# Delta-rule attention and a rational MoE on one core: units of 512 elements become pairs of 1024, in one tile with two buffers

## The chip, the cores and the metric

The kernel runs on one core of a Trainium2 chip. The metric is the device time of one execution in microseconds (us), taken as the median of several executions. A profiled execution gives the trace that is read here. The engines are PE (matrix products), DVE (elementwise work), ACT (elementwise functions), POOL (a second elementwise engine) and SP, which issues most DMA transfers. Each engine works through its own list of instructions in order; an instruction that waits for a semaphore holds everything behind it on its engine.

## The reference

The attention part is a delta rule over 768 steps for 4 batches of 8 heads of 48 dimensions, in float32. Its output, reshaped to 3072 tokens of 384, goes through one layer with a rational function:

```python
for t in range(S):
    kt, vt, bt = (k_n[:, :, t], v[:, :, t], beta[:, :, t, None])
    y[:, :, t] = np.einsum('bhd,bhde->bhe', q[:, :, t], state)
    v_old = np.einsum('bhde,bhd->bhe', state, kt)
    state = state + bt[:, :, :, None] * np.einsum('bhd,bhe->bhde', kt, vt - v_old)
...
h = x @ w_in                       # 384 x 2048
P = a[0] + a[1] * h + a[2] * h2 + a[3] * h3
Q = 1.0 + np.abs(b[0]) * np.abs(h) + np.abs(b[1]) * h2
g = P / (Q + 1e-06)
return (g @ w_out).astype(np.float32)   # 2048 x 384
```

The two weight matrices arrive as 64-bit words.

## The kernel before, in words

**Stages.** Up to about 150 us the kernel loads the weights and computes the first attention chunk. `load_in` and `load_out` call `to_f32` (L305 to L325) for each group of 256 or 192 columns: a DMA into a staging tile that shares buffers with the tiles `mw`, `mu` and `mr`, ACT Abs (L316), POOL min and max (L317), DVE shift and mask (L318) and two DVE merges (L325). After that each weight is split into two float16 parts (`split16`, L226 to L232).

**Units.** The attention runs in 12 chunks of 64 steps. A chunk yields 256 tokens, and its MoE work is cut into 8 units of 256 of the 2048 hidden columns, so that there are 96 units. A unit is a set of tiles of 128 partitions by 512 elements:

- `hidden(n)`: 18 products of 128x256 on PE (L808) into one PSUM bank, tile `ph`; the pool `ps_h` has two such banks.
- `numerator(n)`: ACT Abs into `mr` (L826) and ACT Identity into `mu` (L828), both from `ph`; DVE `mw` from `mr` and `ph` (L830); ACT Abs of `mw` (L831); DVE `mu` times `ph` (L832) and the last step of the polynomial (L833).
- `quotient(n)`: ACT Ln (L841) and Exp (L842) into `mr`, the reciprocal of the denominator; DVE `mg` first part (L844); DVE `mw` times that part, written into the PSUM tile `ph` of the *next* unit (L845); DVE the remainder into `mu` (L846); POOL `mg` second part, the product of `mu` and `mr` (L847).
- `accumulate(n)`: 12 products of 128x384 on PE (L862). After the eighth unit of a chunk the sums are copied out (L876) and sent (L884).

**Order.** In the program the loop of `kernel` issues numerator(n), quotient(n-1), a step of the attention, accumulate(n-2) and hidden(n+1). `in_order` ties the six DVE operations of the units to one another in that order, so DVE's list holds L830, L832, L833 of unit n and then L844, L845, L846 of unit n-1. All else is placed by the framework's planner, which puts attention instructions between them where its own time estimate finds room. The attention of chunk c+1 to c+4 runs beside the units of chunk c; it ends before the units do, and the last units run with nothing beside them.

**Buffers.** `mr`, `mu`, `mw` and `mg` have three buffers each: the tile of unit n is the tile of unit n-3 again. Writing into a buffer waits for the last reader of what was there.

Of the kernel before, what the change touches and what calls it, by code (L numbers as in the profile page):

```python
# [36 lines left out]
def kernel(  # L37
# [271 lines left out]
    def to_f32(t, src, nm, keep=MIN_NORMAL):

        n = t.shape[-1]
        st = staged([P, n, 2], U32, "ws" + nm)
# [4 lines left out]
        nc.gpsimd.tensor_scalar(a, a, 3.0e38, keep, op0=ALU.min, op1=ALU.max)  # L317
        nc.vector.tensor_scalar(  # L318
            t, a.bitcast(U32), 3, KEEP, op0=ALU.logical_shift_left, op1=ALU.bitwise_and
        )  # L320
        for word, scalar, in1, op0, op1 in (
            (wh, 0xC0000000, t, ALU.bitwise_and, ALU.bitwise_or),
            (wl, 29, t, ALU.logical_shift_right, ALU.bitwise_or),
        ):
            nc.vector.scalar_tensor_tensor(out=t, in0=word, scalar=scalar, in1=in1, op0=op0, op1=op1)  # L325
# [714 lines left out]
```

## Time and profile before

| what | value |
|---|---|
| median of 3 runs | 843.07 us (842.95 to 843.18) |
| profiled execution, its own time | 849.25 us |
| its span on the core | 845.5 us |
| granted PE clock, mean | 0.944 |
| DVE, PE, ACT, POOL busy | 88%, 74%, 73%, 40% of the span |
| first numerator (L830 of unit 0) | starts at 150.29 us |
| L830 of unit 72 | starts at 719.16 us |
| last DVE operation of a unit (L846 of unit 95) | starts at 837.33 us, takes 0.75 |

Rows of the trace read as follows: in a group, the line in the source, the engine, the operation, the tiles written and read, the shape, and the count; then the busy time, the mean duration in ns, and the idle time of the engine just before these instructions with what ended it. In a timeline, the start in us, the duration, the engine and the operation, and in brackets the idle time before it. The table of windows gives, for stretches of the span, each engine's busy time with its number of instructions in brackets, PE's granted clock, the share of the DMA engines that was busy and the rate.

### The profile page before, as it was taken

Reading aid. Unit: us, or ns where it says so; the run is one execution under the profiler, and the core shown is the slowest. Engines: PE = TensorE matmul, PEld = TensorE weight load, DVE = VectorE, ACT = ScalarE, POOL = GpSimd, SP = SyncE. Lnnn points to the kernel's source line nnn. Section 1 sums busy time; section 2 is a strip of 40 time slices with the busy share of each in tenths; the row PEclk is TensorE's granted clock in tenths of the full one; section 3 lists DMA queues with packets and bytes.
Section 4 is the critical chain, followed back from the end, with each engine's and each line's share of the span. In section 5 each row is a group of like instructions: output and inputs, shape, how many; then the busy total and the mean of one; then the engine's idle time right before and its main releaser. Section 6 shows DMA issues by size and latency. Waiting matters only on the chain.

```text
span 845.5 us, 23179 instructions
## 1 busy us (share of the span) xinstructions
PE 627.7 (74%) x9264; PEld 493.8 (58%) x9264; DVE 740.2 (88%) x1405; ACT 617.1 (73%) x1278; POOL 338.1 (40%) x322
## 2 busy tenths in 40 slices
PE   0330346778778777866978988789789789999995
PEld 0220344666566666755866866667567667786662
DVE  5999896688879778987998999989988799998996
ACT  4866658768667675866966968768668768788873
POOL 6545754334435333253433433432433332222232
PEclk9999996898989898989999999989899999999999
DMA  8998979769979879999599399696597674300000
GB/s 237 249 212 170 225 155 170 123 140 169 157 130 165 146 120 191 146 140 183 93 145 187 71 176 150 119 193 105 98 167 111 110 103 80 76 2 21 1 19 19
DMA packets 466507, 111.46 MB, mean 132 GB/s; under 512 B 431328, under 2 KB 463072, under 8 KB 466400
## 3 DMA queue, kind: packets, MB, share of 16 engines
q1 hardware_dynamic: 464224, 108.83, 71.3%
q8 instruction: 72, 1.18, 0.6%
q10 hardware_dynamic: 2176, 1.17, 0.5%
q14 instruction: 35, 0.29, 0.1%
HBM read 40.47 MB, written 26.23 MB: 79 GB/s over the span
## 4 chain that ended last, share of the span: by engine, by line
DVE 34%; PE 19%; DMA 17%; SPq 11%; ACT 10%; issue 7%; POOL 1%; ACTq 0%; DVEq 0%; POOLq 0%
PE ph L808 7%; PE po L862 5%; DVE ph L845 4%; DVE w_out L325 4%; DVE mg L844 3%; DVE mw L830 3%; DVE mu L833 3%; DVE mu L832 3%; SPq L119 3%; PE pu L401 2%; DMA tq<-xdq 2%; DMA gd<-g 2%; DMA tk<-xdk 2%; SPq L475 2%; DVE mu L846 2%
## 5 line engine op out<-in xcount | busy, mean ns | idle before, releaser
L862 PE MATMUL po<-w_out,mg 128*128 128x384 f16 x1152 | 226.5, 339 | 33.3 <-DVE mg L844 20.9
L847 POOL TENSOR_TENSOR mg<-mu,mr 128x512 f16<-128x512 f32 x96 | 124.8, 1300 | 258.1 <-DVE mu L846 203.8
L808 PE MATMUL ph<-xT,w_in 128*128 128x256 f16 x1728 | 216.3, 280 | 14.1 <-DVE mu L846 11.2
L808 PEld LDWEIGHTS <-w_in 128*128 128x128 f16 x1728 | 169.8, 101 | 51.1 <-DVE mu L846 14.4
L862 PEld LDWEIGHTS <-mg 128*128 128x128 f16 x1152 | 109.5, 101 | 103.4 <-DVE mg L844 27.7
L401 PEld LDWEIGHTS <-kbd 128*128 128x128 f16 x1680 | 66.7, 109 | 47.8 <-issue 43.3
L830 DVE SCALAR_TENSOR_TENSOR mw<-mr,msc,ph 128x512 f32<-128x512 f32 x96 | 71.1, 741 | 22.1 <-ACT mu L828 21.9
L831 ACT ACTIVATE mw<-mw 128x512 f32<-128x512 f32 x96 | 60.4, 629 | 39.7 <-DVE mw L830 39.2
L845 DVE SCALAR_TENSOR_TENSOR ph<-mw,msc,mg 128x512 f32<-128x512 f32 x96 | 81.4, 848 | 1.0
L844 DVE SCALAR_TENSOR_TENSOR mg<-mu,msc,mr 128x512 f16<-128x512 f32 x96 | 81.1, 844 | 0.0
L826 ACT ACTIVATE mr<-ph,msc 128x512 f32<-128x512 f32 x96 | 65.2, 679 | 18.7 <-PE ph L808 6.9
L828 ACT ACTIVATE mu<-ph,coef,msc 128x512 f32<-128x512 f32 x96 | 74.2, 773 | 0.0
L846 DVE SCALAR_TENSOR_TENSOR mu<-mu,msc,ph 128x512 f32<-128x512 f32 x96 | 71.1, 741 | 1.4
L833 DVE SCALAR_TENSOR_TENSOR mu<-mu,msc,ph 128x512 f32<-128x512 f32 x96 | 70.7, 736 | 1.0
L841 ACT ACTIVATE mr<-mw,msc 128x512 f32<-128x512 f32 x96 | 69.2, 721 | 1.7
L401 PE MATMUL pu<-z,ebd 128*128 128x48 f16 x1728 | 54.9, 185 | 18.1 <-DVE z L232 13.5
L401 PEld LDWEIGHTS <-ebd 128*128 128x128 f16 x1728 | 53.9, 98 | 21.7 <-issue 19.4
L832 DVE TENSOR_TENSOR mu<-ph,mu 128x512 f32<-128x512 f32 x96 | 65.5, 682 | 0.0
L842 ACT ACTIVATE mr<-mr 128x512 f32<-128x512 f32 x96 | 60.3, 628 | 1.3
L401 PEld LDWEIGHTS <-wbd 128*128 128x128 f16 x1152 | 37.7, 99 | 35.9 <-issue 34.8
L230 POOL TENSOR_TENSOR mm<-m,mm 128x1024 f16<-128x1024 f32 x12 | 29.2, 2436 | 73.6 <-ACT mm L226 64.5
L401 PE MATMUL pm<-tq,kbd 128*128 128x64 f16 x576 | 27.0, 220 | 20.1 <-DMA tq<-xdq 18.3
(195 smaller groups left out, 1195.0 us busy)
## 6 DMA issues: line engine op xcount, KB each, us to landing
...
```

The source lines that it names most:

```text
L401: nc.tensor.matmul(dst[p][:, h], head(bd, lp, p * H + h), head(rt, rp, p * H + h), start=start and n == 0 and h == 0, stop=stop and n == l ...
L808: nc.tensor.matmul(ph[:, i], w_in[:, f2, wp, cc, i * P : (i + 1) * P], x[:, xp, cc], start=k == 0, stop=k == 3 * NCC - 1,)
L828: nc.scalar.activation(u, ph, AF.Identity, scale=A3, bias=a2)
L830: in_order(nc.vector.scalar_tensor_tensor(out=w, in0=z, scalar=B0, in1=ph, op0=ALU.add, op1=ALU.mult))
L832: in_order(nc.vector.tensor_mul(u, ph, u))
L833: in_order(nc.vector.scalar_tensor_tensor(out=u, in0=u, scalar=A1, in1=ph, op0=ALU.add, op1=ALU.mult))
L841: nc.scalar.activation(r, w, AF.Ln, bias=Q0)
L844: in_order(nc.vector.scalar_tensor_tensor(out=g[:, 0], in0=u, scalar=A0, in1=r, op0=ALU.add, op1=ALU.mult))
L845: in_order(nc.vector.scalar_tensor_tensor(out=t, in0=w, scalar=Q0, in1=g[:, 0], op0=ALU.add, op1=ALU.mult))
L846: in_order(nc.vector.scalar_tensor_tensor(out=u, in0=u, scalar=A0, in1=t, op0=ALU.add, op1=ALU.subtract))
L847: nc.gpsimd.tensor_mul(g[:, 1], u, r)
L862: nc.tensor.matmul(po[p], g[:, gp, i, p * P : (p + 1) * P], w_out[:, f2, wp, i], start=f2 == lo and i == 0 and k == 0, stop=f2 == hi - 1 a ...
```

## The change

Two units become one pair, from the first product on. There are 48 pairs. `hidden(m)` makes 36 products into one PSUM tile of two banks, and `ps_h` has one such tile instead of two of one bank. The elementwise steps of a pair are 128x1024, so each is one instruction where it was two. `mr`, `mu` and `mw` are parts of one tile `mx` of 3x1024 elements with two buffers (12 KB per partition each), and `mg` has two buffers. `L845`'s product is written into `mw` in SBUF (now L838) instead of the PSUM tile of the next unit. Ln and Exp are issued with the numerator. The products of both units of pair m-1 are issued at the end of step m. The scales of the columns are per pair, so per 512 columns. The weights' words come in groups of 768 columns, are converted in place, and their staging tile is `mx`. The second half of each `w_out` unit is split by ACT and DVE, not by ACT and POOL.

New lines answer to old ones thus: the products of L808 and L862 become L797 and L855; L826, L828, L830, L831, L832, L833 become L819, L820, L821, L822, L823, L824; L841, L842 become L825, L826; L844, L845, L846, L847 become L837, L838, L839, L840. (So L826 is Abs before and Exp after.) Lines of the attention stand 13 lower (L655 is L642, L705 is L692).

```diff
-    MB = 3
+    MB = 2
-    ps_h = ctx.enter_context(tc.tile_pool(name="ps_h", bufs=2, space=PSUM))
+    ps_h = ctx.enter_context(tc.tile_pool(name="ps_h", bufs=1, space=PSUM))
...
+    NS = NU // 2
-    sw = cpool.tile([P, 4, NU], F32, name="sw")
-    tab = cpool.tile([P, 6, NU], F32, name="tab")
+    sw = cpool.tile([P, 4, NS], F32, name="sw")
+    tab = cpool.tile([P, 6, NS], F32, name="tab")
...
-    def to_f32(t, src, nm, keep=MIN_NORMAL):
+    def to_f32(t, srcs, nm, keep=MIN_NORMAL):
-        st = staged([P, n, 2], U32, "ws" + nm)
-        nc.sync.dma_start(out=st.rearrange("p f w -> p (f w)"), in_=src)
-        a = sb.tile([P, n], F32, tag="mg", name="wa" + nm, bufs=MB)
...
+        st = sb.tile([P, len(srcs), n, 2], U32, tag="mx", name="ws" + nm, bufs=MB)
+        for h, src in enumerate(srcs):
+            w, x = st[:, h], t[:, h]
+            nc.sync.dma_start(out=w.rearrange("p (a f) w -> p a (f w)", a=src.shape[1]), in_=src)
+            wl, wh = w[..., 0], w[..., 1]
+            nc.scalar.activation(x.bitcast(F32), wh.bitcast(F32), AF.Abs)
+            nc.gpsimd.tensor_scalar(x.bitcast(F32), x.bitcast(F32), 3.0e38, keep, op0=ALU.min, op1=ALU.max)
+            nc.vector.tensor_scalar(x, x, 3, KEEP, op0=ALU.logical_shift_left, op1=ALU.bitwise_and)
+            for word, scalar, op0 in ((wh, 0xC0000000, ALU.bitwise_and), (wl, 29, ALU.logical_shift_right)):
+                nc.vector.scalar_tensor_tensor(out=x, in0=word, scalar=scalar, in1=x, op0=op0, op1=ALU.bitwise_or)
...
     def load_out(...):
-        for j in range(2):
-            if j == 0:
-                split16((w_out[:, i, 0, j], w_out[:, i, 1, j]), to[j].bitcast(F32), ss[:, 1:2])
-            else:
-                scaled(to[j].bitcast(F32), ss[:, 1:2])
-                split16((w_out[:, i, 0, j], w_out[:, i, 1, j]), to[j].bitcast(F32), eng=nc.gpsimd)
+        for i in us:
+            split16((w_out[:, i, 0], w_out[:, i, 1]), t[:, i % 2], ss[:, 1:2])
...
-    def hidden(n):
-        ph = ps_h.tile([P, 2, TG], F32, tag="h", name=f"ph_{n}")
+    def hidden(m):
+        ph = ps_h.tile([P, 2, 2, TG], F32, tag="h", name=f"ph_{m}")
+        for h in range(2):
+            for i in range(2):
...
     def numerator(...):
-        r = z = sb.tile([P, 2, TG], F32, tag="mr", name=f"mr{n}", bufs=MB)
-        u = sb.tile([P, 2, TG], F32, tag="mu", name=f"mu{n}", bufs=MB)
-        w = sb.tile([P, 2, TG], F32, tag="mw", name=f"mw{n}", bufs=MB)
+        x = d["x"] = sb.tile([P, 3, 4 * TG], F32, tag="mx", name=f"mx{m}", bufs=MB)
+        u, w, r = (x[:, i] for i in range(3))
...
+        nc.scalar.activation(r, w, AF.Ln, bias=Q0)
+        nc.scalar.activation(r, r, AF.Exp, scale=-1.0)

     def quotient(...):
-        t = unit[min(n + 1, NCH * NU - 1)]["ph"]
-        nc.scalar.activation(r, w, AF.Ln, bias=Q0)
-        nc.scalar.activation(r, r, AF.Exp, scale=-1.0)
-        g = sb.tile([P, 2, 2, TG], F16, tag="mg", name=f"mg{n}", bufs=MB)
-        in_order(nc.vector.scalar_tensor_tensor(out=t, in0=w, scalar=Q0, in1=g[:, 0], op0=ALU.add, op1=ALU.mult))
-        in_order(nc.vector.scalar_tensor_tensor(out=u, in0=u, scalar=A0, in1=t, op0=ALU.add, op1=ALU.subtract))
-        nc.gpsimd.tensor_mul(g[:, 1], u, r)
+        g = d["g"] = sb.tile([P, 2, 2, 2, TG], F16, tag="mg", name=f"mg{m}", bufs=2)
+        in_order(nc.vector.scalar_tensor_tensor(out=w, in0=w, scalar=Q0, in1=g0, op0=ALU.add, op1=ALU.mult))
+        in_order(nc.vector.scalar_tensor_tensor(out=u, in0=u, scalar=A0, in1=w, op0=ALU.add, op1=ALU.subtract))
+        nc.gpsimd.tensor_mul(g1, u, r)
...
-    for n in range(N + 2):
-        c, j = divmod(n, NU)
-        if n < N:
-            numerator(n)
-        if 0 <= n - 1 < N:
-            quotient(n - 1)
-        attention(*divmod(n + SHIFT, NU))
-        if 0 <= n - 2 < N:
-            accumulate(n - 2)
-        if n + 1 < N:
-            hidden(n + 1)
+    for m in range(N // 2 + 1):
+        if m < N // 2:
+            numerator(m)
+        if m > 0:
+            quotient(m - 1)
+        attention(*divmod(2 * m + SHIFT, NU))
+        if m + 1 < N // 2:
+            hidden(m + 1)
+        attention(*divmod(2 * m + 1 + SHIFT, NU))
+        if m > 0:
+            accumulate(2 * m - 2)
+            accumulate(2 * m - 1)
...
+    nc = _bacc.Bacc("TRN2", target_bir_lowering=False, num_devices=1, dynamic_dma_scratch_size=2048)
```

The order of instructions moves with it. In the rows below a name is a tile with its number, what stands ahead of `<-` is written, `msc` and `coef` are scales, and the brackets name the engines whose semaphores the instruction waits for.

DVE at the end of the program, where no attention is left. Before:

```order
L830 SCALAR_TENSOR_TENSOR mw90_13819<-mr90_13815,msc_11_13589,ph_90_13796 128x512 [waits PE_49,Activation_49]
L832 TENSOR_TENSOR mu90_13817<-ph_90_13796,mu90_13817 128x512 [waits Pool_49]
L833 SCALAR_TENSOR_TENSOR mu90_13817<-mu90_13817,msc_11_13589,ph_90_13796 128x512 [waits DVE_49]
L844 SCALAR_TENSOR_TENSOR mg89_13826<-mu89_13765,msc_11_13589,mr89_13763 128x512
L845 SCALAR_TENSOR_TENSOR ph_90_13796<-mw89_13767,msc_11_13589,mg89_13826 128x512 [waits DVE_49]
L846 SCALAR_TENSOR_TENSOR mu89_13765<-mu89_13765,msc_11_13589,ph_90_13796 128x512 [waits DVE_49]
L830 SCALAR_TENSOR_TENSOR mw91_13868<-mr91_13864,msc_11_13589,ph_91_13845 128x512 [waits PE_49,Activation_49]
```

and with the change:

```order
L821 SCALAR_TENSOR_TENSOR mx45_12531<-mx45_12531,msc_11_12350,ph_45_12465 128x1024 [waits PE_49,Activation_49,Pool_49]
L823 TENSOR_TENSOR mx45_12531<-ph_45_12465,mx45_12531 128x1024
L824 SCALAR_TENSOR_TENSOR mx45_12531<-mx45_12531,msc_11_12350,ph_45_12465 128x1024 [waits DVE_49]
L837 SCALAR_TENSOR_TENSOR mg44_12540<-mx44_12451,msc_11_12350 128x1024
L838 SCALAR_TENSOR_TENSOR mx44_12451<-mx44_12451,msc_11_12350,mg44_12540 128x1024 [waits DVE_49]
L839 SCALAR_TENSOR_TENSOR mx44_12451<-mx44_12451,msc_11_12350 128x1024 [waits DVE_49]
L821 SCALAR_TENSOR_TENSOR mx46_12608<-mx46_12608,msc_11_12350,ph_46_12545 128x1024 [waits PE_49,Activation_49,Pool_49]
```

The step of three operations for the new tile and three for the tile before stays; L830 waited for PE and ACT, and L821, which opens the step, waits for POOL too.

ACT at the same place. Before, unit 92 and the opening of unit 93:

```order
L826 ACTIVATE mr92_13911<-ph_92_13892,msc_11_13589 128x512 [waits PE_49,Pool_49]
L828 ACTIVATE mu92_13913<-ph_92_13892,coef_99,msc_11_13589 128x512
L831 ACTIVATE mw92_13915<-mw92_13915 128x512 [waits DVE_49]
L841 ACTIVATE mr92_13911<-mw92_13915,msc_11_13589 128x512 [waits Activation_49]
L842 ACTIVATE mr92_13911<-mr92_13911 128x512 [waits Activation_49]
L826 ACTIVATE mr93_13958<-ph_93_13939,msc_11_13589 128x512 [waits PE_49,Pool_49]
L828 ACTIVATE mu93_13960<-ph_93_13939,coef_99,msc_11_13589 128x512
```

and with the change, pair 46 and the opening of pair 47:

```order
L819 ACTIVATE mx46_12608<-ph_46_12545,msc_11_12350 128x1024 [waits PE_49,Pool_49]
L820 ACTIVATE mx46_12608<-ph_46_12545,coef_99,msc_11_12350 128x1024
L822 ACTIVATE mx46_12608<-mx46_12608 128x1024 [waits DVE_49]
L825 ACTIVATE mx46_12608<-mx46_12608,msc_11_12350 128x1024 [waits Activation_49]
L826 ACTIVATE mx46_12608<-mx46_12608 128x1024 [waits Activation_49]
L819 ACTIVATE mx47_12683<-ph_47_12622,msc_11_12350 128x1024 [waits PE_49,Pool_49]
L820 ACTIVATE mx47_12683<-ph_47_12622,coef_99,msc_11_12350 128x1024
```

The order of the five functions is the same. L826 of unit 92 writes the buffer of `mr` that unit 89 used, and the POOL operation that it waits for is L847 of unit 89. L819 of pair 46 writes the buffer of `mx` that pair 44 used, and the POOL operation that it waits for is L840 of pair 44, whose DVE input (L839 of pair 44) stands in DVE's list directly ahead of L821 of pair 46.

DVE in the middle of the program, with attention between (`pr`, `wt0`, `wh`, `S16`, `z`, `sh`, `m32` are its tiles). Before:

```order
L833 SCALAR_TENSOR_TENSOR mu8_3392<-mu8_3392,msc_1_3087,ph_8_3371 128x512 [waits DVE_49]
L844 SCALAR_TENSOR_TENSOR mg7_3401<-mu7_3237,msc_0_1329,mr7_3235 128x512
L571 TENSOR_REDUCE wt0_111<-pr_3_2504 128x2x4x4 [waits DVE_49]
L845 SCALAR_TENSOR_TENSOR ph_8_3371<-mw7_3239,msc_0_1329,mg7_3401 128x512 [waits DVE_49]
L561 TENSOR_TENSOR pr_3_2504<-gb_3_2329,wt0_111 128x512 [waits DVE_49]
L232 SCALAR_TENSOR_TENSOR z_2_1_3406<-pu_2_3144,zmask_85,z_2_1_3406 128x768 [waits Activation_49]
L846 SCALAR_TENSOR_TENSOR mu7_3237<-mu7_3237,msc_0_1329,ph_8_3371 128x512 [waits DVE_49]
L830 SCALAR_TENSOR_TENSOR mw9_3521<-mr9_3517,msc_1_3087,ph_9_3498 128x512
L832 TENSOR_TENSOR mu9_3519<-ph_9_3498,mu9_3519 128x512 [waits Pool_49]
```

and with the change:

```order
L824 SCALAR_TENSOR_TENSOR mx8_3919<-mx8_3919,msc_2_3647,ph_8_3750 128x1024 [waits DVE_49]
L837 SCALAR_TENSOR_TENSOR mg7_3928<-mx7_3678,msc_1_2608 128x1024
L565 SCALAR_TENSOR_TENSOR wh_5_4450<-wt0_111,wh_5_4450 128x256 [waits DVE_49]
L692 SCALAR_TENSOR_TENSOR S16_133<-pd_3_4297,sc_3_1907,S16_133 128x768 [waits PE_49]
L838 SCALAR_TENSOR_TENSOR mx7_3678<-mx7_3678,msc_1_2608,mg7_3928 128x1024 [waits DVE_49]
L232 SCALAR_TENSOR_TENSOR sh_4_4494<-S16_133,sc_4_2959,sh_4_4494 128x768 [waits Activation_49]
L839 SCALAR_TENSOR_TENSOR mx7_3678<-mx7_3678,msc_1_2608 128x1024 [waits DVE_49]
L642 TENSOR_TENSOR m32_5_4226<-pm_5_4177,mask_91 128x1024 [waits DMAHW2_49,DMAHW1_49,PE_49]
L821 SCALAR_TENSOR_TENSOR mx9_4280<-mx9_4280,msc_2_3647,ph_9_4013 128x1024 [waits Activation_49,Pool_49]
L823 TENSOR_TENSOR mx9_4280<-ph_9_4013,mx9_4280 128x1024
```

Attention instructions stand between L821 of a pair and L839 of the pair before as well as between that L839 and the next L821.

More of the change, by code (lines that the diff above doesn't have):

```diff
@@ L785, in scalars @@
         if lo == 0:
-            d["m"] = sb.tile([P, 6, NU], F32, tag="msc", name=f"msc_{c}")
+            d["m"] = sb.tile([P, 6, NS], F32, tag="msc", name=f"msc_{c}")
         nc.vector.tensor_mul(d["m"][:, :, u], tab[:, :, u], sf.unsqueeze(2).broadcast_to([P, 6, hi - lo]))
         d["ikap"][lo] = hi, ikap
-    unit = {}
     acc = {}
@@ L798 @@
     obs = {}
-    def hidden(n):
-        c, f2 = divmod(n, NU)
+    both = {}
+    def hidden(m):
+        c, s2 = divmod(m, NS)
         x = toks[c]["x"]
-        ph = ps_h.tile([P, 2, TG], F32, tag="h", name=f"ph_{n}")
-        for i in range(2):
-            k = 0
-            for cc in range(NCC):
-                for wp, xp in PASSES:
-                    nc.tensor.matmul(
-                        ph[:, i],
-                        w_in[:, f2, wp, cc, i * P : (i + 1) * P],
-                        x[:, xp, cc],
-                        start=k == 0,
-                        stop=k == 3 * NCC - 1,
-                    )
-                    k += 1
-        unit[n] = {"ph": ph}
@@ L818, in numerator @@
-    def numerator(n):
-        c, f2 = divmod(n, NU)
-        d = unit[n]
-        A3, B1, A1, B0, A0, Q0 = (toks[c]["m"][:, i, f2 : f2 + 1] for i in range(6))
-        ph = d["ph"]
-        r = z = sb.tile([P, 2, TG], F32, tag="mr", name=f"mr{n}", bufs=MB)
-        nc.scalar.activation(z, ph, AF.Abs, scale=B1)
-        u = sb.tile([P, 2, TG], F32, tag="mu", name=f"mu{n}", bufs=MB)
+        ph = ps_h.tile([P, 2, 2, TG], F32, tag="h", name=f"ph_{m}")
+        for h in range(2):
+            for i in range(2):
+                k = 0
+                for cc in range(NCC):
+                    for wp, xp in PASSES:
+                        nc.tensor.matmul(
+                            ph[:, h, i],
+                            w_in[:, 2 * s2 + h, wp, cc, i * P : (i + 1) * P],
+                            x[:, xp, cc],
+                            start=k == 0,
+                            stop=k == 3 * NCC - 1,
+                        )
+                        k += 1
@@ L828, in numerator, with flat @@
+        both[m] = {"ph": ph}
+    def flat(t):
+        return t.rearrange("p i a t -> p (i a t)")
+    def numerator(m):
+        c, s2 = divmod(m, NS)
+        d = both[m]
+        A3, B1, A1, B0, A0, Q0 = (toks[c]["m"][:, x, s2 : s2 + 1] for x in range(6))
+        ph = flat(d.pop("ph"))
+        x = d["x"] = sb.tile([P, 3, 4 * TG], F32, tag="mx", name=f"mx{m}", bufs=MB)
+        u, w, r = (x[:, i] for i in range(3))
+        nc.scalar.activation(r, ph, AF.Abs, scale=B1)
         nc.scalar.activation(u, ph, AF.Identity, scale=A3, bias=a2)
-        w = sb.tile([P, 2, TG], F32, tag="mw", name=f"mw{n}", bufs=MB)
@@ L986 @@
                 back(0, j)
-            elif what == "w":
+            elif what == "w" and j < NS:
                 load_in(j)
-            elif what == "o":
+            elif what == "o" and j < NS:
                 weights_out(j)
```

116 lines of the change are left out of this document (52 added, 64 removed).

## The prediction

> **What bounds the kernel now.** I read the page's busy shares, the table of windows by stage, then the timeline of the last stretch, where only units run.
>
> ```profile
> PE 627.7 (74%) x9264; PEld 493.8 (58%) x9264; DVE 740.2 (88%) x1405; ACT 617.1 (73%) x1278; POOL 338.1 (40%) x322
> 0.00:150.00 150.00, 48.64 (x731) 40.73 (x732) 127.52 (x347) 99.52 (x263) 86.31 (x122) 0.95 0.91 201
> 220.00:700.00 480.00, 396.59 (x6229) 314.23 (x6226) 428.12 (x751) 353.10 (x690) 184.62 (x145) 0.94 0.83 140
> 784.90:829.00 44.10, 41.82 (x309) 29.10 (x307) 42.90 (x69) 36.95 (x70) 12.76 (x10) 1.00 0.04 10
> ```
>
> DVE is the fullest engine throughout: 85% of the first 150 us, 89% of the middle, 97% at the end, where POOL is busy for 29%. The rate of units follows from the starts of L826:
>
> ```profile
> 220.00:700.00 480.00, 42.18 (x62) 0.94 0.83 140
> 784.93 0.67 ACT L826 ACTIVATE mr<-ph,msc 128x512 f32<-128x512 f32 x1
> 829.03 0.67 ACT L826 ACTIVATE mr<-ph,msc 128x512 f32<-128x512 f32 x1
> ```
>
> In the middle 62 units take 480 us, 15.5 us for two; at the end ten units lie between these two starts, 8.8 us for two. One round of DVE there:
>
> ```profile
> 790.76 0.75 DVE L846 SCALAR_TENSOR_TENSOR mu<-mu,msc,ph 128x512 f32<-128x512 f32 x1
> 791.42 0.74 DVE L830 SCALAR_TENSOR_TENSOR mw<-mr,msc,ph 128x512 f32<-128x512 f32 x1
> 792.08 0.68 DVE L832 TENSOR_TENSOR mu<-ph,mu 128x512 f32<-128x512 f32 x1
> 792.81 0.74 DVE L833 SCALAR_TENSOR_TENSOR mu<-mu,msc,ph 128x512 f32<-128x512 f32 x1
> 793.47 0.75 DVE L844 SCALAR_TENSOR_TENSOR mg<-mu,msc,mr 128x512 f16<-128x512 f32 x1
> 794.25 0.76 DVE L845 SCALAR_TENSOR_TENSOR ph<-mw,msc,mg 128x512 f32<-128x512 f32 x1
> 795.04 0.75 DVE L846 SCALAR_TENSOR_TENSOR mu<-mu,msc,ph 128x512 f32<-128x512 f32 x1
> ```
>
> L846 to L846 is 4.28 us without a gap: with three buffers POOL and ACT run ahead, and DVE alone sets the pace.
>
> **The change part by part.** *Wider DVE operations.*
>
> ```profile
> L832 DVE TENSOR_TENSOR mu<-ph,mu 128x512 f32<-128x512 f32 x96 | 65.5, 682 | 0.0
> L655 DVE TENSOR_TENSOR m<-pm,mask 128x1024 f32<-128x1024 f32 x12 | 14.6, 1216 | 10.6 <-PE pm L401 10.6
> ```
>
> The second 512 elements cost 1216 - 682 = 0.53 us, the first about 0.71 start to start. Six operations per pair are 4.28 + 6 x 0.53 = 7.48 us instead of 8.56: 1.08 us less per pair, 52 us over 48 pairs, if DVE still set the pace. From the start of the numerator's first to the end of the quotient's last operation it is 3.62 (791.42 to 795.04) + 0.75 + 6 x 0.53 = 7.57 us.
>
> [...]
>
> *Two buffers for a pair.* L819 of pair m+1 writes the `mx` that pair m-1 still holds until POOL's L840 has read it (the rows of pair 46). L840 needs L839 of pair m-1, which stands on DVE behind pair m's numerator. L821 of m+1 then waits for ACT's L819 and L820. So DVE round, POOL and ACT come one after another, where three buffers let them overlap. The prices:
>
> ```profile
> 785.50 0.77 ACT L828 ACTIVATE mu<-ph,coef,msc 128x512 f32<-128x512 f32 x1
> 785.68 0.75 DVE L846 SCALAR_TENSOR_TENSOR mu<-mu,msc,ph 128x512 f32<-128x512 f32 x1
> 786.35 0.74 DVE L830 SCALAR_TENSOR_TENSOR mw<-mr,msc,ph 128x512 f32<-128x512 f32 x1
> 786.60 1.27 POOL L847 TENSOR_TENSOR mg<-mu,mr 128x512 f16<-128x512 f32 x1 [3.69 <-ACT kp L761]
> L230 POOL TENSOR_TENSOR mm<-m,mm 128x1024 f16<-128x1024 f32 x12 | 29.2, 2436 | 73.6 <-ACT mm L226 64.5
> L230 POOL TENSOR_TENSOR kn<-q,kn 128x768 f16<-128x768 f32 x12 | 20.4, 1699 | 9.9 <-ACT kn L226 9.6 <-DMA gb<-gd 0.2
> L516 ACT ACTIVATE g<-pg 128x1024 f32<-128x1024 f32 x12 | 12.3, 1023 | 6.6 <-PE pg L401 5.5 <-POOL nrm L494 1.0
> ```
>
> DVE to POOL is 786.60 - 786.43 = 0.17. L840 at 1024: 2.13 by the line through 1.27 at 512 and 1.70 at 768, 2.54 by doubling; I take 2.34, close to L230's 2436 ns. POOL to ACT as DVE to POOL, 0.17. ACT: L516's 1023 less L826's 0.67 is 0.35 for the second half, so L819 holds ACT for 0.57 + 0.35 = 0.92 (784.93 to 785.50) and L820 takes 0.77 + 0.35 = 1.12; doubled these would be 1.14 and 1.54. ACT to DVE 0.08 (786.27 to 786.35). Loop: 7.57 + 0.17 + 2.34 + 0.17 + 0.92 + 1.12 + 0.08 = **12.4 us** (12.2 to 13.2) against 8.8. DVE would sit idle for 4.8 us of each.
>
> *Behind the waiting L819* stand on ACT the attention's casts and splits (L226, L228) and copies; PE's products for `pu` and DVE's `z` wait for those. L824 is the last reader of the only `ph`, so hidden(m+1) starts there:
>
> ```profile
> 795.94 2.13 PE L808 MATMUL ph<-xT,w_in 128*128 128x256 f16 x18 [0.19 <-DVE kp L780]
> ```
>
> 36 products are 4.27 us, hidden under the quotient, POOL and its latencies (3.9 + 2.7). At the end that holds, so the single PSUM tile and later products cost nothing; uncovered it is a rival. Fewer ACT and POOL instructions save nothing beyond what the loop's prices hold, since both engines wait within it: ACT is at 74%, POOL at 38% in the middle.
>
> *Start (to the first numerator).*
>
> ```profile
> L325 DVE SCALAR_TENSOR_TENSOR w_out<-wso,w_out 128x192 uint32<-128x192 uint32 x56 | 24.3, 449 | 0.4
> L325 DVE SCALAR_TENSOR_TENSOR w_out<-wsi,w_out 128x256 uint32<-128x256 uint32 x48 | 21.8, 469 | 0.3
> L318 DVE TENSOR_SCALAR w_out<-wai 128x256 uint32<-128x256 uint32 x24 | 10.6, 441 | 4.7 <-POOL wai L317 4.7
> L318 DVE TENSOR_SCALAR w_out<-wao 128x192 uint32<-128x192 uint32 x28 | 10.4, 373 | 0.0
> ```
>
> Some 160 instructions (67 us) become 32 of about 0.95 and 16 of 0.56 at 768 elements, 39 us. The 28 us shrink by overlapping ends (L846's 0.75 against 0.66 to the next start: 0.09 x 112 = 10), and the `w_out` split moved from POOL adds 384 elements to each of eight DVE operations, 0.4 x 8 = 3: 15 net, up to 20 if fewer ends overlap. Scales per pair drop some 0.15 us operations, which is within that. But the first numerator also follows a chain through the attention's PE and ACT steps and the gate, in which 22 of the 150 us leave DVE idle already; how much of the saving reaches its end the trace doesn't show, so I take nearer the lower third, -6 (-20 if all counts; +3 if two staging buffers, with transfers of 786 KB instead of 256 and DMA 91% busy, delay loads).
>
> *Pairs 1 to 35.* From L830 of unit 2 to that of unit 72:
>
> ```profile
> 164.60 0.75 DVE L830 SCALAR_TENSOR_TENSOR mw<-mr,msc,ph 128x512 f32<-128x512 f32 x1 [1.52 <-ACT mu L828]
> 719.16 0.75 DVE L830 SCALAR_TENSOR_TENSOR mw<-mr,msc,ph 128x512 f32<-128x512 f32 x1 [1.48 <-ACT mu L828]
> DVE mw L830 <- ACT mu L828: 19.5, 14, 4.2
> DVE m L655 <- PE pm L401: 10.6, 5, 3.7
> DVE ab L545 <- DMA gb<-gd: 7.2, 6, 2.5
> L844 DVE SCALAR_TENSOR_TENSOR mg<-mu,msc,mr 128x512 f16<-128x512 f32 x96 | 81.1, 844 | 0.0
> L845 DVE SCALAR_TENSOR_TENSOR ph<-mw,msc,mg 128x512 f32<-128x512 f32 x96 | 81.4, 848 | 1.0
> L846 DVE SCALAR_TENSOR_TENSOR mu<-mu,msc,ph 128x512 f32<-128x512 f32 x96 | 71.1, 741 | 1.4
> ```
>
> Before: 554.6. After: 35 x 12.4 = 434. The idle 4.8 us can be filled by attention, but 160 of DVE's attention instructions stand within the round (between a pair's L821 and the L839 before it) and lengthen the loop; with their durations (like L655's) they are 74, and where those in the gap exceed it, 8. That gives 516. To it come waits inside the round (in the list of DVE's waits between 160 and 760 us those other than L830's add to some 43 us, L655's and L545's the largest; 43% of the attention's DVE time stands inside the round, so 18; L830's own 19.5 is what the loop now counts), collisions with POOL (L844 and L845, both inputs in SBUF, average 0.1 above L846; three such operations now: 17), and an ACT or POOL late by their own queues (10, an estimate): 561, **+6** (-38 with none of these, +42 with twice as much).
>
> [...]
>
> *Pairs 36 to 47.* Before, 719.16 to 838.08, the last L846's end (next fence): 118.9. After, 11 x 12.4 + the last numerator and quotient 7.6 + a quotient of 3.9 alone + 3 for the last scalars and attention: 151, **+32**.
>
> *The tail.*
>
> ```profile
> 837.33 0.75 DVE L846 SCALAR_TENSOR_TENSOR mu<-mu,msc,ph 128x512 f32<-128x512 f32 x1
> 838.25 1.26 POOL L847 TENSOR_TENSOR mg<-mu,mr 128x512 f16<-128x512 f32 x1 [1.51 <-DVE mu L846]
> 836.80 2.12 PE L862 MATMUL po<-w_out,mg 128*128 128x384 f16 x12 [1.89 <-POOL mg L847]
> ```
>
> POOL is 1.1 longer, and of the last products those that need POOL's part are eight instead of four, 0.18 each: +1 to +3, I take **+3** with the copy behind.
>
> Sum: -6 + 6 + 32 + 3 = **+35**. The profiled execution took 849.25 (span 845.5), 6.2 above the median of 843.07; on the median's scale 843 + 35 = 878.
>
> **The rivals.**
> A, *DVE still sets the pace* (POOL and ACT overlap after all, or the wait on POOL is for an older pair): 52 us saved on units and 6 to 20 at the start, about 780. For it: 97% DVE busy; against: the order of L839, L840, L819, L821, and in the middle DMA, already 83% busy with transfers that don't shrink. Chance 0.06.
> B, *the gap is filled*: attention falls into the idle 4.8 us without lateness (-38), the start keeps its whole -20, the end its +35: about 820 to 838. For it: 428 of 480 us DVE in the middle leaves little idle. Chance 0.11.
> C, *hidden comes late* in PE's queue. PE is busy 396.59 of 480 us, 12.8 per 15.5; 8.5 of that is not hidden. Numerator 3.7 + 4.27 + ACT 2.04 + latencies 0.3 is 10.3, and with three quarters of the others ahead, 6.5, the loop is 16.8: 35 x 16.8 = 588 + 27 for collisions and lateness = 615 against 554.6, +60, about 935. It decides once over 2.1 us of other products stand ahead. Chance 0.10.
> D, the parts cancel, within 0.2%: 0.05.
>
> **How the numbers follow.** The forecast has 0.68, its own range 845 to 912: the bounds leave -14 to +9 around the start's value, -44 to +36 around the middle's, and the loop's -0.2 to +0.8 another -9 to +37 over 46 loops; not all fall together, so I keep some -33 and +34 of them. A, B are faster (0.17), D the same (0.05), forecast and C slower (0.78); 0.2%, 1.7 us, is about what a measurement tells from no change. The range takes in B and the forecast, 830 to 914.
>
> **What would show it.** At the end, L821 starts 12.4 us apart and waits about 4.8 us for ACT, L819 waits for POOL's L840, and DVE's share there falls to about 60%. L840 takes 2.1 to 2.5. L823 takes about 1.2. In the middle two units take 15 to 17 us. If L821 starts 7.5 apart at the end, the loop is wrong; if L819 waits for PE in the middle, C is right; if the first L821 starts before 135 or after 153, the start is.

## The result and the profile after

The changed kernel takes 965.8 us (median of 4 runs, 962.8 to 967.0) against 843.0 us before: 1.146 times, 95% interval 1.142 to 1.149. The direction was forecast; the time lies far above 878 and above the range's 914. The profiled execution has a span of 965.3 us against 845.5, so 119.8 us have to be found.

The page of the kernel after, engines and three groups:

```profile
PE 663.3 (69%) x9264; PEld 518.6 (54%) x9264; DVE 705.9 (73%) x969; ACT 572.1 (59%) x950; POOL 310.8 (32%) x218
L840 POOL TENSOR_TENSOR mg<-mx 128x1024 f16<-128x1024 f32 x48 | 114.2, 2380 | 275.0 <-DVE mx L839 189.3
L821 DVE SCALAR_TENSOR_TENSOR mx<-mx,msc,ph 128x1024 f32<-128x1024 f32 x48 | 61.3, 1278 | 75.3 <-ACT mx L820 65.5
L819 ACT ACTIVATE mx<-ph,msc 128x1024 f32<-128x1024 f32 x48 | 53.3, 1109 | 64.2 <-POOL mg L840 49.3
```

DVE does its work in 436 fewer instructions and 34 us less, and yet its share falls from 88% to 73%: each engine of the loop now waits for another. The table of windows, for the start, pairs 1 to 35 and four pairs of the end:

```profile
0.00:156.00 156.00, 50.45 (x829) 44.12 (x830) 113.81 (x204) 94.51 (x180) 67.60 (x72) 0.93 0.95 201
173.50:800.00 626.50, 481.61 (x7161) 380.58 (x7158) 473.63 (x637) 383.00 (x639) 205.91 (x129) 0.88 0.68 119
904.00:954.00 50.00, 32.54 (x199) 21.10 (x198) 34.95 (x27) 20.51 (x20) 10.27 (x4) 0.88 0.03 8
```

The stretches are cut at DVE's L821 of pairs 0, 1 and 36 and at the last L839; three of these rows and the last one:

```profile
156.24 1.28 DVE L821 SCALAR_TENSOR_TENSOR mx<-mx,msc,ph 128x1024 f32<-128x1024 f32 x1 [0.83 <-ACT mx L820]
173.49 1.27 DVE L821 SCALAR_TENSOR_TENSOR mx<-mx,msc,ph 128x1024 f32<-128x1024 f32 x1
800.14 1.28 DVE L821 SCALAR_TENSOR_TENSOR mx<-mx,msc,ph 128x1024 f32<-128x1024 f32 x1 [1.13 <-ACT mx L820]
952.80 1.28 DVE L839 SCALAR_TENSOR_TENSOR mx<-mx,msc 128x1024 f32<-128x1024 f32 x1
```

| stretch | before | after | difference | forecast |
|---|---|---|---|---|
| to the first numerator | 150.3 | 156.2 | +5.9 | -6 |
| first numerator to that of pair 1 | 14.3 | 17.2 | +2.9 | not counted |
| pairs 1 to 35 | 554.6 | 626.7 | +72.1 | +6 |
| pair 36 to the last DVE operation | 118.9 | 153.9 | +35.0 | +32 |
| tail | 7.4 | 11.2 | +3.8 | +3 |

The end is the loop as forecast. One turn of it, from the timeline of DVE, POOL and ACT:

```profile
928.30 1.28 DVE L821 SCALAR_TENSOR_TENSOR mx<-mx,msc,ph 128x1024 f32<-128x1024 f32 x1 [4.85 <-ACT mx L820]
934.58 1.28 DVE L839 SCALAR_TENSOR_TENSOR mx<-mx,msc 128x1024 f32<-128x1024 f32 x1
936.03 2.35 POOL L840 TENSOR_TENSOR mg<-mx 128x1024 f16<-128x1024 f32 x1 [10.07 <-DVE mx L839]
938.42 1.11 ACT L819 ACTIVATE mx<-ph,msc 128x1024 f32<-128x1024 f32 x1 [5.48 <-POOL mg L840]
939.43 1.20 ACT L820 ACTIVATE mx<-ph,coef,msc 128x1024 f32<-128x1024 f32 x1
940.72 1.28 DVE L821 SCALAR_TENSOR_TENSOR mx<-mx,msc,ph 128x1024 f32<-128x1024 f32 x1 [4.86 <-ACT mx L820]
```

7.56 of DVE, 0.17, 2.35 of POOL, 0.04, 2.21 of ACT, 0.09: 12.42 us, against 12.4 in the forecast, with 4.86 us of DVE waiting.

In the middle a pair takes 17.9 us where 16.0 were forecast. The same chain there, its parts summed over pairs 1 to 35 from the starts and ends of these instructions (of the forecast's terms, the 10 for an ACT or POOL late by their own queues stands in the fourth row, the 8 for attention in the gap in the sixth):

```
part of the loop                       forecast   measured (us, 35 pairs)
L821(m) to the end of L839(m-1), DVE      374        354.8
to POOL's start                             6         20.5
POOL L840                                  82         82.8
POOL's end to the start of L819            16         78.2
L819 and L820, ACT                         71         77.1
to the next L821                           11         13.2
sum                                       560        626.7
```

The round with its attention work, collisions and waits came out 19 us cheaper than I had it. What is missing is the step from POOL to ACT: 2.2 us per pair instead of 0.5. One such place, POOL's product of pair 25 and then ACT's list until L819 of pair 27:

```profile
646.61 2.37 POOL L840 TENSOR_TENSOR mg<-mx 128x1024 f16<-128x1024 f32 x1 [6.72 <-DVE mx L839]
...
648.51 0.37 ACT L748 ACTIVATE kp<-kp 128x1 f32<-128x1 f32 x1
648.78 0.88 ACT L228 ACTIVATE z<-pu,zmask 128x768 f16<-128x768 f32 x1
649.74 0.20 ACT L764 ACTIVATE kp<-kp 128x1 f32<-128x1 f32 x1
649.98 0.20 ACT L765 ACTIVATE kp<-kp 128x1 f32<-128x1 f32 x1
650.39 1.02 ACT L503 ACTIVATE g<-pg 128x1024 f32<-128x1024 f32 x1 [0.21 <-PE pg L388]
651.31 1.11 ACT L819 ACTIVATE mx<-ph,msc 128x1024 f32<-128x1024 f32 x1
```

POOL is done at 648.98, and L819 starts 2.3 us later with no idle time before it: attention work stands ahead of it in ACT's list. That is why the view of what L819 waits for, taken from 173 to 800 us, shows only little of it:

```profile
L819 ACT ACTIVATE mx<-ph,msc x35: 1094/1108/1132, 198.5 to 797.9; 128x1024 f32<-128x1024 f32 x35
...
  POOL mg L840: 13.9, 5
  DVE sc L604: 5.1, 2
  DVE msc L774: 4.7, 2
  PE ph L797: 1.1, 1
```

In 26 of the 35 pairs the instruction before L819 ended after both POOL and PE; in 8 POOL was the last of the three, in one PE. In three of the 8 and one of the 26, L819 then still waited for scales that DVE computes (`sc` and `msc` in the view), 6.3 us in all. Of the 78 us between POOL's end and L819, ACT was busy with attention work for 47 and idle for 31: for 23 in front of attention instructions that waited for their own inputs, for 7.5 in front of L819 itself. In pairs 2 and 34 hidden, too, ended 7.2 and 7.4 us after POOL, so that PE alone would have held L819 nearly as long there.

### The profile page after: what moved, and what is told of

It reads as the page before. It is cut to its first block, busy times and chain, and to the rows that moved or that the text cites. A ratio compares the mean times of both kernels' runs of the same rounds, so it can differ in the third digit from the quotient of the medians.

```text
span 965.3 us, 21992 instructions
## 1 busy us (share of the span) xinstructions
PE 663.3 (69%) x9264; PEld 518.6 (54%) x9264; DVE 705.9 (73%) x969; ACT 572.1 (59%) x950; POOL 310.8 (32%) x218
## 4 chain that ended last, share of the span: by engine, by line
DVE 31%; DMA 20%; ACT 14%; SPq 13%; PE 11%; issue 5%; POOL 4%; DVEq 0%; ACTq 0%; POOLq 0%
PE ph L797 5%; DVE mx L821 4%; DMA gd<-g 3%; ACT mx L820 3%; ACT mx L819 3%; DVE mx L824 3%; DMA gb<-gd 3%; POOL mg L840 3%; DVE mx L823 3%; DVE mx L838 3%; SPq L119 3%; SPq L593 2%; DVE mg L837 2%; DMA v<-in_v_dram 2%; DVE mx L839 2%
## 5 line engine op out<-in xcount | busy, mean ns | idle before, releaser
L797 PE MATMUL ph<-xT,w_in 128*128 128x256 f16 x1728 | 231.6, 299 | 63.3 <-DVE mx L824 61.2
L855 PE MATMUL po<-w_out,mg 128*128 128x384 f16 x1152 | 222.2, 346 | 27.6 <-POOL mg L840 22.7
L797 PEld LDWEIGHTS <-w_in 128*128 128x128 f16 x1728 | 181.6, 107 | 103.6 <-DVE mx L824 57.5
L840 POOL TENSOR_TENSOR mg<-mx 128x1024 f16<-128x1024 f32 x48 | 114.2, 2380 | 275.0 <-DVE mx L839 189.3
L855 PEld LDWEIGHTS <-mg 128*128 128x128 f16 x1152 | 115.0, 103 | 106.9 <-POOL mg L840 26.8
L821 DVE SCALAR_TENSOR_TENSOR mx<-mx,msc,ph 128x1024 f32<-128x1024 f32 x48 | 61.3, 1278 | 75.3 <-ACT mx L820 65.5
L819 ACT ACTIVATE mx<-ph,msc 128x1024 f32<-128x1024 f32 x48 | 53.3, 1109 | 64.2 <-POOL mg L840 49.3
L822 ACT ACTIVATE mx<-mx 128x1024 f32<-128x1024 f32 x48 | 50.7, 1057 | 34.8 <-DVE mx L821 34.6
L838 DVE SCALAR_TENSOR_TENSOR mx<-mx,msc,mg 128x1024 f32<-128x1024 f32 x48 | 69.0, 1439 | 0.5
L839 DVE SCALAR_TENSOR_TENSOR mx<-mx,msc 128x1024 f32<-128x1024 f32 x48 | 66.5, 1385 | 0.7
L837 DVE SCALAR_TENSOR_TENSOR mg<-mx,msc 128x1024 f16<-128x1024 f32 x48 | 64.4, 1343 | 0.0
L824 DVE SCALAR_TENSOR_TENSOR mx<-mx,msc,ph 128x1024 f32<-128x1024 f32 x48 | 61.0, 1272 | 0.6
L823 DVE TENSOR_TENSOR mx<-ph,mx 128x1024 f32<-128x1024 f32 x48 | 58.4, 1216 | 0.0
L820 ACT ACTIVATE mx<-ph,coef,msc 128x1024 f32<-128x1024 f32 x48 | 57.5, 1198 | 0.0
L825 ACT ACTIVATE mx<-mx,msc 128x1024 f32<-128x1024 f32 x48 | 55.1, 1147 | 0.8
L230 POOL TENSOR_TENSOR mm<-m,mm 128x1024 f16<-128x1024 f32 x12 | 29.6, 2468 | 78.2 <-ACT mm L226 73.7
L826 ACT ACTIVATE mx<-mx 128x1024 f32<-128x1024 f32 x48 | 50.5, 1053 | 0.7
L230 POOL TENSOR_TENSOR kn<-k,kn 128x768 f16<-128x768 f32 x12 | 22.2, 1847 | 64.5 <-ACT kn L226 58.5
```

Of the source, the lines that this page charges most:

```text
L797: nc.tensor.matmul(ph[:, h, i], w_in[:, 2 * s2 + h, wp, cc, i * P : (i + 1) * P], x[:, xp, cc], start=k == 0, stop=k == 3 * NCC - 1,)
L819: nc.scalar.activation(r, ph, AF.Abs, scale=B1)
L820: nc.scalar.activation(u, ph, AF.Identity, scale=A3, bias=a2)
L821: in_order(nc.vector.scalar_tensor_tensor(out=w, in0=r, scalar=B0, in1=ph, op0=ALU.add, op1=ALU.mult))
L823: in_order(nc.vector.tensor_mul(u, ph, u))
L824: in_order(nc.vector.scalar_tensor_tensor(out=u, in0=u, scalar=A1, in1=ph, op0=ALU.add, op1=ALU.mult))
```

## The experiments

Theory 1: a tile of two buffers puts DVE's round, POOL and ACT in series; in the middle ACT's in-order list is added to it. Theory 2: the single PSUM tile makes hidden late on PE. Theory 3: the wider operations collide with POOL. The runs are compared with the kernel before on the same chip, where it took 847.5 to 849.8 us, 5 to 7 more than beside the change. The change was not run again there, so a difference in whole times between it and an experiment is uncertain by about as much; the columns by stage come from one trace of each kernel.

| kernel | us | ratio, 95% interval | first numerator | middle, us per pair | end, us per pair |
|---|---|---|---|---|---|
| before (profile shown ahead) | 843.0 | 1 | 150.3 | 15.84 | 8.8 |
| the change | 965.8 | 1.146 (1.142 to 1.149) | 156.2 | 17.90 | 12.42 |
| two512 | 1069.5 | 1.256 (1.245 to 1.267) | 160.2 | 19.86 | 14.46 |
| pool_free | 931.6 | 1.098 (1.090 to 1.106) | 154.9 | 17.30 | 10.17 |
| r_third | 918.0 | 1.081 (1.073 to 1.088) | 163.5 | 16.70 | 10.23 |
| skew0 | 892.9 | 1.050 (1.044 to 1.057) | 155.5 | 16.28 | 10.3 to 11.7 |
| act_extra | 987.7 | 1.165 (1.160 to 1.170) | 155.8 | 18.51 | 12.4 to 12.8 |
| skew0_short | 880.6 | 1.042 (1.034 to 1.050) | 152.9 | 16.45 | 8.5 to 10.9 |
| four512 | 853.1 | 1.008 (1.005 to 1.010) | 151.9 | 16.07 | 8.8 |
| words768 | 855.2 | 1.010 (1.006 to 1.014) | 151.8 | 16.20 | 8.8 |
| scratch | 849.1 | 1.004 (1.000 to 1.007) | 150.0 | 15.85 | 8.8 |

The middle is from the numerator of pair 1 to that of pair 36; the end is the distance of the last numerators, two units for the kernels of 512 (8.8 is a mean over the last ten units).

### Two buffers, without the wide tiles

```diff
-    STAGES = (("mw", MB), ("mu", MB), ("mr", MB))
+    STAGES = (("mw", 2), ("mu", 2), ("mr", 2))
-        r = z = sb.tile([P, 2, TG], F32, tag="mr", name=f"mr{n}", bufs=MB)
+        r = z = sb.tile([P, 2, TG], F32, tag="mr", name=f"mr{n}", bufs=2)
...
```

> The kernel before with two buffers instead of three for mr, mu and mw (units of 512 as before, two PSUM banks, words in small groups). Theory 1 (a tile that waits for its own POOL product puts DVE's round, POOL and ACT in series): in the last stretch a unit takes 4.3 + 0.2 + 1.3 + 0.2 + 0.6 + 0.8 + 0.1 = 7.3 us, so 14.6 for two, against 8.8; the last 24 units cost 60 to 70 us more and the middle 1 to 4 us per two units, in all 930 to 1050. Theory 2 (the single PSUM tile makes the hidden products late) and theory 3 (1024-wide operations collide with POOL) both leave this kernel near before, 843 to 860.

1069.5 us. The timelines of DVE and ACT at the end:

```profile
1042.79 0.75 DVE L846 SCALAR_TENSOR_TENSOR mu<-mu,msc,ph 128x512 f32<-128x512 f32 x1
1045.00 0.69 ACT L826 ACTIVATE mr<-ph,msc 128x512 f32<-128x512 f32 x1 [3.01 <-POOL mg L847]
1046.39 0.75 DVE L830 SCALAR_TENSOR_TENSOR mw<-mr,msc,ph 128x512 f32<-128x512 f32 x1 [2.86 <-ACT mu L828]
1053.62 0.75 DVE L830 SCALAR_TENSOR_TENSOR mw<-mr,msc,ph 128x512 f32<-128x512 f32 x1 [2.85 <-ACT mu L828]
```

7.23 us per unit for the 7.3 expected. In all it took 20 us more than the 1050 that theory 1 gave at most. The excess lies at the start, which theory 1 did not count: the first numerator comes 10 us later than before, and 9 more pass up to the numerator of unit 2; the words' staging, which shares these tiles, has six instead of nine here. One buffer less in each of the three, with nothing else of the change, costs more than the change does; theories 2 and 3 leave no room for that. Per two units the short tiles pay POOL, ACT and the latencies twice (2.85 us from L846's end to the next L830, 5.7 for two, against 4.86 in the change), so wide tiles soften the loop rather than make it.

### POOL off the loop

```diff
-        nc.gpsimd.tensor_mul(g1, u, r)
+        nc.gpsimd.memset(g1, 0.0)
```

> The changed kernel with POOL writing zeros to the second part of mg instead of multiplying mu by mr (that part of the quotient is left out): POOL no longer reads mx, so the next pair's L819 waits for DVE's L839. Theory 1: at the end 10.3 us from L821 to L821 instead of 12.4 (numerator 3.7, hidden 4.2, ACT 2.2, latencies 0.2; the round with ACT alone would be 9.9); in the middle ACT's own list is last in most pairs, so only 0.5 to 1.5 us per pair come back; in all 890 to 925. Theory 2: the middle stays within 10 us, in all 935 to 945. Theory 3: the middle's operations lose their collisions, 0.2 us for each of three, and nothing else: 930 to 945.

931.6 us, 6.6 above what theory 1 gave at most. The end is 10.17 us, and there L819 now waits for PE:

```profile
899.02 1.28 DVE L821 SCALAR_TENSOR_TENSOR mx<-mx,msc,ph 128x1024 f32<-128x1024 f32 x1 [2.60 <-ACT mx L820]
906.95 1.11 ACT L819 ACTIVATE mx<-ph,msc 128x1024 f32<-128x1024 f32 x1 [3.29 <-PE ph L797]
909.19 1.28 DVE L821 SCALAR_TENSOR_TENSOR mx<-mx,msc,ph 128x1024 f32<-128x1024 f32 x1 [2.60 <-ACT mx L820]
```

So the single PSUM tile has a floor of its own (numerator, hidden, ACT) behind that of the buffers. In the middle only 0.6 us per pair come back of the 3.0 that POOL and the way to it take there: ACT's list is nearly as late without POOL. These 21 us are also what theory 3 asked for, but not by its mechanism: the quotient's three operations are no shorter, although POOL's zeros take only 0.95 us. DVE's groups from 173 to 779 us, first of the change and then of this kernel:

```profile
L837 DVE SCALAR_TENSOR_TENSOR mg<-mx,msc 128x1024 f16<-128x1024 f32 x34 | 46.6, 1369 | 0.0
L838 DVE SCALAR_TENSOR_TENSOR mx<-mx,msc,mg 128x1024 f32<-128x1024 f32 x34 | 49.1, 1445 | 0.2
L839 DVE SCALAR_TENSOR_TENSOR mx<-mx,msc 128x1024 f32<-128x1024 f32 x34 | 48.5, 1427 | 0.3
```

```profile
L837 DVE SCALAR_TENSOR_TENSOR mg<-mx,msc 128x1024 f16<-128x1024 f32 x35 | 48.4, 1384 | 0.0
L838 DVE SCALAR_TENSOR_TENSOR mx<-mx,msc,mg 128x1024 f32<-128x1024 f32 x35 | 48.6, 1390 | 0.0
L839 DVE SCALAR_TENSOR_TENSOR mx<-mx,msc 128x1024 f32<-128x1024 f32 x35 | 53.2, 1519 | 0.2
```

### A third buffer for r

```diff
-        x = d["x"] = sb.tile([P, 3, 4 * TG], F32, tag="mx", name=f"mx{m}", bufs=MB)
-        u, w, r = (x[:, i] for i in range(3))
+        u, w, r = d["x"] = [sb.tile([P, 4 * TG], F32, tag=tag, name=f"{tag}{m}", bufs=bufs)
+                            for tag, bufs in (("mu", 2), ("mw", 2), ("mr", 3))]
...
-        in_order(nc.vector.scalar_tensor_tensor(out=u, in0=u, scalar=A0, in1=w, op0=ALU.add, op1=ALU.subtract))
-        nc.gpsimd.tensor_mul(g1, u, r)
+        in_order(nc.vector.scalar_tensor_tensor(out=w, in0=u, scalar=A0, in1=w, op0=ALU.add, op1=ALU.subtract))
+        nc.gpsimd.tensor_mul(g1, w, r)
```

> The changed kernel with u, w and r in tiles of their own, three buffers for r, the remainder (L839) written over w, and words staged in pieces of 256 and 384 columns instead of 768. L819 and L820 then wait for no POOL product. Theory 1: at the end 10.3 us per pair; the middle 15.5 to 17 instead of 17.9; first numerator at 148 to 156; in all 880 to 920. Theory 2: the middle stays at 17.5 to 18, in all 940. Theory 3: as theory 2.

918.0 us: end 10.23, middle 16.70, as theory 1 has it. The start missed: here, with small words in seven staging tiles, the first numerator comes at 163.5, and why is not settled.

### The quotient behind its own numerator

```diff
-        if m > 0:
-            quotient(m - 1)
+        if m < N // 2:
+            quotient(m)
```

> The changed kernel with each pair's quotient issued directly behind its own numerator instead of behind the next pair's: the POOL product then ends long before the tile is written again. Theory 1: the loop is numerator 3.7, hidden 4.2, ACT 2.2 and latencies, 10.3 at the end (a wait of about 1 us for Exp before L837 is inside it); the middle 14 to 16.5 per pair; in all 850 to 900. Theory 2: hidden stays on the path in the middle, 17 to 18 per pair, in all 930 to 950. Theory 3: the middle stays at 17 to 18.

892.9 us, the best of the paired kernels, still 5% behind the kernel before. The order alone takes 73 us of the loss away with the same two buffers. In some turns of the end, as in this one of 11.67 us, hidden starts behind products of the pair before on PE, and ACT waits for it:

```profile
848.96 4.45 PE L855 MATMUL po<-w_out,mg 128*128 128x384 f16 x16 [1.98 <-POOL mg L840]
853.25 4.09 PE L797 MATMUL ph<-xT,w_in 128*128 128x256 f16 x36
857.44 1.11 ACT L819 ACTIVATE mx<-ph,msc 128x1024 f32<-128x1024 f32 x1 [4.73 <-PE ph L797]
859.74 1.28 DVE L821 SCALAR_TENSOR_TENSOR mx<-mx,msc,ph 128x1024 f32<-128x1024 f32 x1 [3.07 <-ACT mx L820]
```

### More work ahead of L819 on ACT

```diff
+        junk = sb.tile([P, 4 * TG], F16, tag="junk", name=f"junk{m}", bufs=1)
+        nc.scalar.copy(junk, ph)
         nc.scalar.activation(r, ph, AF.Abs, scale=B1)
```

> The changed kernel with one more ACT operation per pair: a copy of ph (128x1024) into a tile that nobody reads, issued right ahead of L819. Theory 1 (in the middle ACT's own list of attention work, not POOL, decides when L819 starts): at the end ACT is idle 5.5 us while it waits for POOL, so the copy is free there and L821 stays 12.4 us apart; in the middle its 1.05 us counts in the 26 of 35 pairs in which ACT was last, 15 to 35 us, in all 975 to 1000. Rival (POOL's product or PE's hidden decides in the middle too, and ACT has slack ahead of L819): the middle grows by less than 8 us, in all 963 to 973.

987.7 us, 22 above the change. The numerators of pairs 1 and 36 (L823 here), and the copy and the function behind it (L819 of the change) at the end:

```profile
172.95 1.27 DVE L823 SCALAR_TENSOR_TENSOR mx<-mx,msc,ph 128x1024 f32<-128x1024 f32 x1
820.69 1.28 DVE L823 SCALAR_TENSOR_TENSOR mx<-mx,msc,ph 128x1024 f32<-128x1024 f32 x1 [1.85 <-ACT mx L822]
...
960.94 1.01 ACT L820 CAST junk<-ph 128x1024 f16<-128x1024 f32 x1 [3.29 <-PE ph L797]
963.13 1.11 ACT L821 ACTIVATE mx<-ph,msc 128x1024 f32<-128x1024 f32 x1 [1.18 <-POOL mg L842]
```

The middle grows by 21.1 us, 0.60 per pair of the copy's 1.01. At the end the turn shown stays at 12.42, since the function behind the copy still waits for POOL; in the two turns before it the copy, which waits for hidden, ends later than POOL, and they take 12.69 and 12.80. From pair 36 to the last DVE operation the copy costs 4 us in twelve pairs. Where ACT waits for POOL the work is nearly free, and in the middle it is paid in more than half of its length: ACT's list stands last in most pairs there. That is the direct evidence for the missing term.

### What holds the middle once the loop is gone

skew0 with hidden cut to a third of its products:

```diff
-                    for wp, xp in PASSES:
+                    for wp, xp in PASSES[:1]:
...
```

> The kernel with the quotient directly behind its numerator, and hidden cut to 12 of its 36 products (the products of the small float16 parts of x and w_in are left out). Theory 1a (with the wait for POOL gone, the one PSUM tile is the next bound: numerator, hidden, ACT, numerator): the loop at the end falls from 10.3 by 2.8 to 7.5, so that DVE with its wait for Exp sets it, 8.6 to 8.9 us per pair; the middle falls from 16.3 to 14 to 15; in all 815 to 850. Theory 1b (DVE's own wait for Exp or ACT's list holds the loop): the end stays above 10, the middle falls by under 0.7 us per pair, in all 870 to 890.

880.6 us. The end falls to 8.5 to 9.3 where hidden comes at once, and stays at 10.6 to 10.9 where it stands behind products on PE, so neither theory has the end right; the middle does not fall (16.45), and the whole lies in theory 1b's range. So neither the PSUM tile nor hidden sets skew0's middle.

The attention nearly alone, by leaving out the units of pairs 0 to 43:

```diff
-        if m < N // 2:
+        if 44 <= m < N // 2:
             numerator(m)
...
```

> The changed kernel with the units of the last chunk alone (pairs 44 to 47; hidden, numerator, quotient and products of all others are left out), so that the attention runs by itself after the start. Theory F (the attention's own chain through its engines and DMAs sets a floor for the middle, near what before takes, 63 us a chunk): a chunk, from one L642 to the next, takes 52 to 64 us, and the span is 690 to 800. Theory G (the attention has slack, and the middle hangs on the units' loop and on who stands ahead of whom): a chunk takes under 45 us, and the span is under 620.

The product m32 (L642) comes once per chunk; its rows for the fourth and the last chunk, and the window between:

```profile
222.86 1.23 DVE L642 TENSOR_TENSOR m<-pm,mask 128x1024 f32<-128x1024 f32 x1 [0.73 <-PE pm L388]
620.06 1.23 DVE L642 TENSOR_TENSOR m<-pm,mask 128x1024 f32<-128x1024 f32 x1 [3.20 <-PE pm L388]
220.00:620.00 400.00, 188.64 (x4356) 180.22 (x4356) 161.22 (x358) 161.47 (x358) 94.04 (x82) 0.62 0.93 155
```

49.7 us per chunk, between what the two theories gave and nearer to the first; the one run took 739.7 us, inside the first's range. With the DMA engines 93% busy, the attention takes 12.4 us for each pair even without units. Before takes 15.84, so units that cost nothing would save some 3.4 us per pair there; this is an estimate, since PE's granted clock was 0.62 in this window and 0.94 before. What holds skew0 at 16.3 between that floor and its own loop is not settled; no single wait in it is large (from 173 to 779 us, 38 pairs, the largest of DVE's are L837's for Exp and all those of L821, 21 us each).

### The start, the buffers and the DMA scratch alone

words768 is the kernel before with the change's `to_f32` (groups of 768, in place, two staging tiles of 6 KB):

> The kernel before (units of 512) with only the weights' words changed: groups of 768 columns, converted in place, two staging tiles of their own. Start by DVE's work (theory S1): 15 to 20 us less of it, so the first numerator at 132 to 142 instead of 150 and in all 825 to 836. Start by DMA and the attention's chain (theory S2): first numerator at 147 to 154, in all 840 to 848. Staging too short (theory S3): first numerator at 155 to 163, in all 848 to 858. The middle and the end stay at 15.8 and 8.8 us for two units under each.

```profile
0.00:151.80 151.80, 48.66 (x731) 40.84 (x731) 112.85 (x213) 92.35 (x209) 71.85 (x78) 0.63 0.90 196
151.84 0.74 DVE L819 SCALAR_TENSOR_TENSOR mw<-mr,msc,ph 128x512 f32<-128x512 f32 x1
```

DVE's work falls by 14.7 us (127.52 before) and the first numerator comes no earlier: theory S2 for the start. The middle, which was to stay, is 0.36 per pair slower, so that the whole, 855.2, is 7 above S2's range.

four512 is the kernel before with `MB = 4`:

> The kernel before with four buffers instead of three for mr, mu, mw, mg and the words' staging. Theory 1: with three DVE sets the pace at the end already, so 8.6 to 8.8 us for two units stay; the waits for ACT in the middle (19.5 us) shrink by a part and the start, with twelve staging tiles instead of nine, comes 0 to 6 us earlier: 830 to 843. Rival (the units were still short of buffers): the end falls under 8.5 for two, in all under 828.

853.1 us where 830 to 843 were expected: no gain, 0.8% slower; the end is unchanged, so before wasn't short of buffers.

scratch is the kernel before with only `dynamic_dma_scratch_size=2048`, which the prediction passed over:

> The kernel before with nothing changed but the scratch for dynamic DMA, 2048 as in the change (the lists of instructions are the same on all engines). Theory A (it costs nothing): within 0.4% of before. Theory B (the two kernels of 512 with it, four buffers and large words, are 0.8 to 1.0% slower because of it): 0.6 to 1.2% slower.

1.004 (1.000 to 1.007): the median is within theory A, and the interval reaches into B's 0.6%. This 0.4% would be about half of what four512 and words768 lose, which have the smaller scratch too; the rest isn't settled.

No run has pairs with three buffers and two PSUM tiles, so what the wider operations alone are worth stays open.

## Why the prediction was wrong

- *The loop of two buffers.* Right in mechanism and size: 12.42 us for 12.4, and L819 waits for POOL at the end. two512 shows that the buffer count alone makes it. The wider DVE operations cost what the rows gave (L821 to L839's end 7.56 for 7.57).
- *Pairs 1 to 35.* Here it failed, by 66 us, in one term: "an ACT or POOL late by their own queues (10, an estimate)". It came to 87 us: 72 between POOL and ACT beyond the latency of 6, and 14.5 on the way to POOL, which was busy with other work for 12.5 us there. The waits, the collisions and the round together were 19 too dear, ACT's two functions and the step behind them 8 too cheap. The collisions alone, 17 in the forecast, show in the trace: L837, L838 and L839 took 13.9 us more there than the 1278 ns each that they take undisturbed. All 14 of these rows above 1.4 us stood beside attention work on POOL (L230, L489), so they stayed without POOL's product: 16 us in pool_free. Beside L840 only the L838 at 949.52 us was long, 3.24. The estimate of 10 rested on no row. The prediction named what stands behind L819 on ACT, and never counted what stands ahead of it: over these pairs the trace has 298 instructions of attention work on ACT between L826 of a pair and L819 of the next, eight or nine per pair. The order was known beforehand, and their rows could have been priced.
- *"Fewer ACT and POOL instructions save nothing"* held, but its reason did not: 74% of ACT busy was read as room. ACT is one serial step of this loop, and work that stands ahead of that step was largely on the path: of the 1.01 us of act_extra's copy 0.60 per pair was paid in the middle.
- *Rival C* came nearest in time (935) by the wrong cause, so its nearness is luck: PE's hidden was last in one of 35 pairs and close behind ACT in two more, and ACT's list did what C ascribed to PE's. The single PSUM tile is a bound only once POOL is off the loop (10.2 to 10.3 at the end of three kernels).
- *Rivals A and B* fell. B assumed that attention fills DVE's idle 4.8 us without lateness. From the end of L839 to the next L821 DVE had 272 us over pairs 1 to 35; attention filled 130 of them, and 142 (4.1 per pair) stayed idle: with ACT and POOL late the gap itself was 272 instead of the forecast's 186.
- *The start.* -6 forecast, +5.9 measured; by the prediction's own sign (a first L821 after 153) it was wrong. DVE's work fell by 13.7 us (127.52 to 113.81), close to the 15 worked out, and none of it reached the first numerator; words768 shows the same without pairs. Of the 4.4 us by which the change is still later than words768, the first pair's 18 more products (2.1) and two wider ACT operations (0.43 each: 1.12 and 1.20 us against 0.69 and 0.77 before) would explain 3.0, an estimate; no run separates them. The 2.9 us from the first numerator to the second weren't in the sum.
- *The end and the tail.* +35 and +4 against +32 and +3.
- *The range.* Doubling all three lateness terms (18, 17 and 10) would give +51 for the middle; the +42 that the prediction names, 36 above its +6 as 914 is above 878, is about what doubling the waits and the collisions alone gives. So the one term without a row had no spread upwards.
